# In-place exponentials in PSUM, two-bank PSUM tiles and two chunks per group in an RWKV6 + Hyena kernel

## The chip, the cores and the metric

The kernel runs on one core of a Trainium2 chip. The metric is device time in microseconds (us) of one execution. Every run is compared with runs of the kernel before on the same chip. Executions carry a state: "slow" is a run that is more than 1.5% above the fastest of its kernel; verdicts use the fast runs alone. The engines are PE (matrix multiplies), DVE (VectorE), ACT (ScalarE), POOL (GpSimd) and SP (which issues DMAs here).

## The reference

Stage one is RWKV6 attention with a state; stage two takes its output through a projection, a long convolution in the frequency domain, gates and an output projection. Cut to what matters:

```python
B, H, S, D = 4, 8, 768, 48
for t in range(S):                                    # stage one
    cur = einsum('bhd,bhe->bhde', u[None] * kt, vt)   # the "bonus" of the current step
    y[:, :, t] = einsum('bhd,bhde->bhe', rt, state + cur)
    state = wt[:, :, :, None] * state + einsum('bhd,bhe->bhde', kt, vt)
x = y.transpose(0, 2, 1, 3).reshape(B, S, H * D)      # stage two
x1, x2, x3 = split(x @ w_proj)
x2_conv = irfft(rfft(x2) * rfft(filter_fft))
out = (x1 * x2_conv * x3) @ w_out
```

## The kernel before

Stage one runs on 24 chunks of 128 time steps (six per batch). The kernel declares every step as an operation with a due time, its possible engines and the PSUM banks that it takes. A list scheduler in the kernel (`Plan`) then orders them with estimated durations, chooses the banks, and emits the instructions in that order. Its estimates are a model.

The kernel before uses eight banks of PSUM. It declares six of them as six tiles of one bank, and the last two as one tile `sc`, which only the scores use. Cut to one chunk's start and the state update:

```python
NB = 6
bank = [ps.tile([L, 512], FP32, name=f"bank{i}") for i in range(NB)]
sc = ps.tile([L, 2, HP, L], FP32, name="sc")
# ... cut: csi and csx are cumulative sums of log w by PE, each in a bank of its own
op(f"en{i}", T(i, 1.2), [act(C)], lambda e, bk: nc.scalar.activation(
    out=en[f], in_=bank[bk[f"csi{i}"]][:, 0:C], func=AF.Exp, scale=-1.0), w=[f"en.{f}"], uses=[f"csi{i}"])
op(f"ep{i}", T(i, 1.3), [act(C + HP)], lambda e, bk: nc.scalar.activation(
    out=ep[f], in_=bank[bk[f"csx{i}"]][:, 0:C + HP], func=AF.Exp), w=[f"ep.{f}"], uses=[f"csx{i}"])
op(f"kh{i}", T(i, 1.9), [pool(C), dve(C, True)], lambda e, bk: mul(
    e, kh[f][:, :, 0:D], kl[sl], en[f]), ...)
op(f"qh{i}", T(i, 2.0), [pool(C), dve(C, True)], lambda e, bk: mul(e, qh[f][:, :, 0:D], rl[sl], ep[f]...), ...)
# ... cut: transposes, scores, mt = scores * mask; kv = ident @ S + k v on PE; then the new state:
op(f"su{i}", T(i, 4.9), [dve(HP * D)], lambda e, bk: nc.vector.tensor_mul(
    stt[sn], bank[bk[f"kv{i}"]][:, 0:HP * D]..., ep[f][:, C:C + HP].to_broadcast([L, HP, D])), uses=[f"kv{i}"])
```

## Time and profile before

| | kernel before |
|---|---|
| median of the first runs | 179.68 us (179.07 to 182.61) |
| span in the profile | 179.9 us |
| PE / DVE / ACT / POOL busy | 149.2 / 148.7 / 136.5 / 74.3 us |
| DVE idle | 179.9 - 148.7 = 31.2 us |

The page of the profile: first busy time per engine, then busy tenths in 40 slices of 4.5 us, the shares of the engines in the chain of waits that ended last, and one group of instructions (output from inputs, count, busy us, mean ns, idle before them).

```profile
span 179.9 us, 4559 instructions
## 1 busy us (share of the span) xinstructions
PE 149.2 (83%) x1698; PEld 90.5 (50%) x1698; DVE 148.7 (83%) x290; ACT 136.5 (76%) x304; POOL 74.3 (41%) x87
## 2 busy tenths in 40 slices
PE   0553988197999999998999988679999999998761
...
DVE  3899899548979779999997899976799999639650
...
## 4 chain that ended last, share of the span: by engine, by line
PE 49%; DVE 29%; DMA 9%; issue 7%; ACT 2%; POOL 2%; SPq 1%; DVEq 0%; POOLq 0%; ACTq 0%
...
L621 DVE TENSOR_TENSOR sd<-xT 128x384 bf16<-128x384 bf16 x24 | 10.7, 474 | 2.6 <-ACT xT L282 2.4
```

PE and DVE are both over 80% busy, and the chain of waits hops between them. The slices show where it is not so: at the start and after slice 35. Three windows of 40 us say the same in numbers (columns: start:end, length, busy us and instructions of each engine, granted PE clock, DMA share, GB/s):

```profile
core 0: us, PE busy (x) PEld busy (x) DVE busy (x) ACT busy (x) POOL busy (x), PEclk, DMA share, GB/s
0.00:40.00 40.00, 23.77 (x276) 15.97 (x277) 31.38 (x75) 27.00 (x52) 14.52 (x28) 0.87 0.94 196
40.00:80.00 40.00, 37.96 (x451) 23.34 (x449) 36.37 (x68) 33.40 (x79) 18.57 (x20) 1.00 1.02 197
...
160.00:201.00 41.00, 12.54 (x80) 5.81 (x78) 10.88 (x30) 8.62 (x18) 0.00 (x0) 0.96 0.08 29
```

In the first 40 us PE has only 23.8 us of work and the DMA engines are busy throughout: the start waits for loads. In the last 20 us both engines run down. (The span ends at 179.9, so the last window is half empty.)

### The profile page before, as it was taken

What the parts mean: (1) busy time and instruction counts of PE and PEld (TensorE: products, weight loads), DVE (VectorE), ACT (ScalarE), POOL (GpSimd) and SP (SyncE); (2) the same over time, 40 slices, a digit from 0 to 9 for tenths busy, and PEclk for the clock granted to TensorE, in tenths of its full rate; (3) what the DMA queues carried; (4) which work ended last, traced back from release to release, by engine and by line L of the source; (5) the groups of instructions that cost most, each with busy time, mean ns of one, the idle gap of its engine ahead of it and who ended that gap; (6) DMA issues with size and microseconds to landing.
All of it is one profiled execution on the core that took longest, in us unless ns stands there. A gap on an engine that the chain in (4) does not pass through costs nothing.

```text
span 179.9 us, 4559 instructions
## 1 busy us (share of the span) xinstructions
PE 149.2 (83%) x1698; PEld 90.5 (50%) x1698; DVE 148.7 (83%) x290; ACT 136.5 (76%) x304; POOL 74.3 (41%) x87
## 2 busy tenths in 40 slices
PE   0553988197999999998999988679999999998761
PEld 0433765144665663565556744436656556654230
DVE  3899899548979779999997899976799999639650
ACT  4597795378798796899799974949999968686332
POOL 6055632026453454539423992846650562100000
PEclk9999996569999999999999999969999999999998
DMA  5999999699999899999999984467000001500006
GB/s 113 213 219 183 193 299 212 121 211 215 199 173 206 164 213 182 213 206 190 298 176 187 212 175 95 79 168 219 4 2 4 0 4 64 201 5 0 0 31 231
DMA packets 105046, 26.44 MB, mean 147 GB/s; under 512 B 100288, under 2 KB 104640, under 8 KB 105024
## 3 DMA queue, kind: packets, MB, share of 16 engines
q1 hardware_dynamic: 104224, 24.98, 63.5%
q0 software_dynamic: 800, 1.18, 4.0%
q8 instruction: 13, 0.21, 0.5%
q14 instruction: 9, 0.07, 0.1%
HBM read 22.61 MB, written 4.72 MB: 152 GB/s over the span
## 4 chain that ended last, share of the span: by engine, by line
PE 49%; DVE 29%; DMA 9%; issue 7%; ACT 2%; POOL 2%; SPq 1%; DVEq 0%; POOLq 0%; ACTq 0%
DMA r<-in_r_dram 9%; PE bank L594 9%; PE bank L630 7%; PE bank L703 5%; DVE mt L420 4%; DVE U L661 4%; PE bank L516 4%; DVE y L692 3%; PE bank L391 3%; PE sc L414 3%; PE bank L462 3%; DVE eo L689 2%; PE bank L448 2%; DVE P L661 2%; PE bank L509 2%
## 5 line engine op out<-in xcount | busy, mean ns | idle before, releaser
L420 DVE TENSOR_TENSOR mt<-sc,mask_excl 128x1024 bf16<-128x1024 f32 x24 | 29.2, 1218 | 5.2 <-PE sc L414 5.0
L594 PE MATMUL bank<-xT,wproj 128*128 128x384 bf16 x144 | 28.4, 326 | 0.0
L278 POOL TENSOR_TENSOR kh<-k,en 128x384 bf16<-128x384 f32 x16 | 18.4, 1150 | 23.1 <-ACT en L375 21.7
L278 POOL TENSOR_TENSOR vc<-vb,cc 128x384 bf16<-128x384 bf16 x15 | 12.7, 855 | 33.1 <-DVE cc L404 24.7
L278 POOL TENSOR_TENSOR rk<-r,k 128x384 bf16<-128x384 f32 x16 | 17.3, 1078 | 14.9 <-DMA r<-in_r_dram 14.2
L282 ACT ACTIVATE qk<-bank 128x1024 bf16<-128x1024 bf16 x20 | 20.7, 1033 | 2.5 <-PE bank L391 1.8
L278 POOL TENSOR_TENSOR qh<-r,ep 128x384 bf16<-128x384 f32 x17 | 19.5, 1149 | 3.9 <-ACT ep L378 3.9
L703 PE MATMUL bank<-wout,y 128*128 128x384 bf16 x72 | 14.7, 350 | 3.5 <-DVE y L692 3.4
L357 ACT ACTIVATE lg<-w 128x384 bf16<-128x384 f32 x24 | 12.4, 530 | 6.2 <-DMA w<-in_w_dram 6.2
L282 ACT ACTIVATE xn<-bank 128x192 bf16<-128x192 f32 x48 | 13.8, 344 | 4.1 <-PE bank L462 3.6
L594 PEld LDWEIGHTS <-wproj 128*128 128x128 bf16 x144 | 12.5, 97 | 7.0 <-issue 0.3
L363 PE MATMUL bank<-lg,mask_incl 128*128 128x384 bf16 x24 | 8.7, 364 | 8.6 <-ACT lg L357 8.3
L282 ACT ACTIVATE o<-bank 128x384 f32<-128x384 f32 x24 | 11.3, 511 | 5.6 <-PE bank L703 5.5
L630 PE MATMUL bank<-wproj,sd 128*128 128x384 bf16 x72 | 14.2, 326 | 0.9 <-DVE sd L621 0.9
L611 DVE TENSOR_TENSOR g<-bank,x 128x384 bf16<-128x384 f32 x24 | 12.7, 548 | 2.4 <-ACT ab L282 1.6
L282 ACT ACTIVATE xT<-bank 128x384 bf16<-128x384 bf16 x24 | 12.0, 501 | 2.9 <-PE bank L479 2.8
L282 ACT ACTIVATE ev<-bank 128x384 f32<-128x384 f32 x12 | 5.9, 492 | 10.5 <-PE bank L678 10.5
L282 ACT ACTIVATE X<-bank 128x384 bf16<-128x384 f32 x24 | 11.9, 508 | 2.3 <-PE bank L509 1.1
L282 ACT ACTIVATE x<-bank 128x384 bf16<-128x384 f32 x24 | 11.9, 496 | 1.9 <-PE bank L594 1.6
L375 ACT ACTIVATE en<-bank 128x384 f32<-128x384 f32 x24 | 12.0, 500 | 1.2 <-PE bank L363 1.0
L404 DVE TENSOR_REDUCE cc<-rku 128x8 f32<-128x384 bf16 x24 | 12.8, 542 | 0.0
L621 DVE TENSOR_TENSOR sd<-xT 128x384 bf16<-128x384 bf16 x24 | 10.7, 474 | 2.6 <-ACT xT L282 2.4
(102 smaller groups left out, 371.0 us busy)
## 6 DMA issues: line engine op xcount, KB each, us to landing
w<-in_w_dram SPq DMA_DIRECT2D x24, 192.0 KB, 4.0
k<-in_k_dram SPq DMA_DIRECT2D x24, 192.0 KB, 3.9
r<-in_r_dram SPq DMA_DIRECT2D x24, 192.0 KB, 3.9
v<-in_v_dram SPq DMA_DIRECT2D x24, 192.0 KB, 3.8
out_dram<-o SPq DMA_DIRECT2D x24, 192.0 KB, 2.3
filt<-in_moe_filter_fft_dram SPq DMA_DIRECT2D x1, 1152.0 KB, 7.9
wproj<-in_moe_w_proj_dram POOLq DMA_DIRECT2D x1, 864.0 KB, 13.1
wout<-in_moe_w_out_dram POOLq DMA_DIRECT2D x1, 288.0 KB, 4.8
```

Source lines behind the costliest of these rows:

```text
L278: (nc.vector if e == DVE else nc.gpsimd).tensor_mul(o, a, b)
L282: nc.scalar.activation(out=o, in_=a, func=AF.Copy)
L357: op(f"ln{i}", T(i, 0), [act(C, True)], lambda e, bk: nc.scalar.activation(out=lg[f][:, :, 0:D], in_=wl[sl], func=AF.Ln), r=[f"w.{sl}", "t ...
L375: op(f"en{i}", T(i, 1.2), [act(C)], lambda e, bk: nc.scalar.activation(out=en[f], in_=bank[bk[f"csi{i}"]][:, 0:C], func=AF.Exp, scale=-1.0 ...
L404: op(f"cc{i}", T(i, 2.8), [dve(C)], lambda e, bk: nc.vector.tensor_reduce(out=cc[f], in_=rku[f], axis=AX.X, op=ALU.add), r=[f"rku.{f}"], w ...
L420: op(f"mt{i}", T(i, 4.8), [dve(1024)], lambda e, bk: nc.vector.tensor_mul(mt[s2_], sc.rearrange("p q j t -> p (q j) t"), _mid(mask_excl, H ...
L594: nc.tensor.matmul(p, wproj[:, cb, col0:col0 + L], xT[bx][:, cb, sl], start=(cb == 0), stop=(cb == CB - 1),)
L611: op("c" + n3, d + 0.3, [dve(C)], lambda e, bk: nc.vector.tensor_mul(g[bx][:, fb, sl], bank[bk[n3]][:, 0:HALF], x1[0][:, fb, sl]), r=[f"x1 ...
L621: op(f"sd{b}.{q}.{ti}", d, [dve2(C, True)], lambda e, bk, q=q, fn=fn: fn(sd[q][:, :, sl], lo, hi), r=[f"xT.{bx}.{ti}", f"xT.{bx}.{NT + ti} ...
L630: nc.tensor.matmul(bank[bk[n]][:, 0:C], sd[q][:, cb, ti * L:(ti + 1) * L], wproj[:, cb, C:2 * C], start=(cb == 0), stop=(cb == CB - 1),)
L661: lambda e, bk, o=o, a=a, c=c, fn=fn: fn(tl(o)[:, sl, :], tl(a)[:, sl, :], tl(c)[:, sl, :]),
L703: nc.tensor.matmul(bank[bk[n]][:, 0:C], y[cb][:, ti * L:(ti + 1) * L], wout[:, cb, :], start=(cb == 0), stop=(cb == CB - 1),)
```

## The change

The intent: fewer and larger instructions, and a shorter chain per chunk. Both exponentials become one ACT instruction of 768 elements that writes over the cumulative sums in PSUM. One DVE multiply then reads k's and q's factors from there and takes k and r (`kq`), in place of two multiplies of 384 on POOL or DVE. To let one instruction span two banks, PSUM is declared as four tiles of two banks. Loads and the first elementwise steps take two chunks as a group (the first two groups have one chunk each, the third and all later ones two). For six of the 13 groups the bonus is made by transposes and small matmuls on PE instead of a DVE reduction. Priorities are tuned anew and the projection weights are loaded after chunk 1's logarithm, not chunk 4's. The core of the diff, with cuts marked:

```diff
-    NB = 6
-    bank = [ps.tile([L, 512], FP32, name=f"bank{i}") for i in range(NB)]
-    sc = ps.tile([L, 2, HP, L], FP32, name="sc")
+    bank = [ps.tile([L, 2, 512], FP32, name=f"bank{i}") for i in range(4)]
+    def one(bk, n):                       # a step that needs one bank: one half of a pair
+        i, m = bk[n]
+        return bank[i // 2][:, i % 2, :]
+    def two(bk, n):                       # a step that needs two: a whole pair
+        i, m = bk[n]
+        return bank[i]
# ... cut
+        def exps(e, bk):
+            p = two(bk, f"cs{i}")
+            nc.scalar.activation(out=p[:, :, 0:C], in_=p[:, :, 0:C], func=AF.Exp)
+            nc.scalar.activation(out=phi[f], in_=p[:, 1, C:C + HP], func=AF.Exp)
+        op(f"kq{i}", T(i, O_KH), [dve(2 * C)], lambda e, bk: nc.vector.tensor_mul(
+            kq[f][:, :, :, 0:D], two(bk, f"cs{i}")[:, :, 0:C]..., kr[sl][:, :, q]), ...)
# ... cut
+            op(f"su{i}", T(i, O_SU), [dve(HP * D)], lambda e, bk: nc.vector.tensor_mul(
+                stt[sn], one(bk, f"kv{i}")[:, 0:HP * D]..., phi[f].to_broadcast([L, HP, D])), uses=[f"kv{i}"])
# ... cut: projections, forward transform, outputs in pairs of banks (one eviction of 768); bonus on PE
-PACE = 5.021
-WP, WO, FL = 4, 9, 5
+PACE = 4.317
+WP, WO, FL = 1, 7, 3
```

In the scheduler each of the eight banks still has a time of its own at which it comes free. A step of one bank may take a half of a pair whose other half is in use.

## The prediction

> **What bounds it now.** The span is 179.9 us. By the table of busy times PE is busy 149 us, DVE 149, ACT 136, POOL 74. The chain of waits hops between PE (49%) and DVE (29%). By windows, between 20 and 150 us DVE is over 90% busy in most stretches and PE 92-100%: a co-limited steady state. The losses are at the ends. From 0 to 40 us PE is busy only 24 us and the DMA share is 0.85-0.98. After 160 us DVE is busy 11 of 20 us. In all, DVE is idle 31 us. Part of its busy time is stretching: sums of bf16 tiles in SBUF take 0.35 us at the median but up to 1.15 when POOL runs (mean 0.47 for sd).
>
> **What the change does, by engine** (durations from the groups by form, 384 -> 768 elements interpolated between the 384 and 1024 forms).
> - DVE: kh and qh (15 multiplies on DVE, 33 on POOL) become 24 multiplies of 768 elements on DVE alone, about 0.95 us each: 22.8 us for 9.8. Given back: rku goes from 24 DVE operations to 3, cc from 24 reductions to 7 double ones (12.8 -> 6.5 us), vc and rk from 17 to 4 double ones, paired g. Added: 9 xT copies (0.35 us), 3 rx, 3 qk. sd now reads one operand from PSUM; the Trainium skill ("VectorE: DVE Perf Modes", "The perf-mode tier table") lists tensor_tensor with any PSUM operand at 1x, so I cost it at 0.35 to 0.55 us, not less. Uncontended, DVE work grows some 4 to 8 us; POOL falls from 74 to about 55 us, so stretching shrinks by about as much. Net DVE busy 145-152 us: no relief.
> - ACT: 300 activations become about 205. Two exponentials (0.50+0.52 us) become one of 768 in place (about 0.8) plus a tiny one (about 0.2); pairs of 384 evictions (2x0.50) become one of 768 (about 0.8). ACT busy 136 -> 120-126 us.
> - PE: the same matmuls plus 30 transposes (8 take 0.45 us) and 30 matmuls of 8 columns: +2 to 3 us.
> - POOL no longer stands between the exponentials and the transposes: two POOL multiplies of 1.15 us in series become one DVE multiply. Waits of POOL on en (21.7 us) and on cc (24.7 us) mostly disappear.
> - Dues are spaced 4.32 us per chunk, not 5.02. Exponentials hold a bank pair until the multiply, but all eight banks circulate.
>
> **On the critical path.** No busy engine gets much less work, so the gain must come from idle time: a shorter chain per chunk (about 1.5 us), a faster start, fewer fixed costs, and at the end output matmuls started before the last y (18 now wait for it, 2.8 us). I expect DVE idle to fall from 31 to about 17-20 us: span about 149 + 18 = 167. Against it: the last batch's tail (21 us after its last sums) stays serial.
>
> Predicted 166.5 us, 8 in 10 between 159 and 175. Faster by over 2%: 0.88; within 2%: 0.08; slower: 0.04.
>
> **Right if** the profile shows DVE busy 145-152 at 88% or more of the span, ACT 120-126, POOL about 55; the 768 multiply about 0.95 us; first 40 us with more PE work than 24 us; tail after the last sums no longer than 21 us.
>
> **Wrong if** in-place exponentials run slow in PSUM; bank pairs held from matmul to multiply starve PE; three group buffers delay loads (ACT waiting on w); the delayed second stage of early batches piles up behind the last chunk so that the tail grows; or the throttle cuts the denser PE stream (granted 0.74 between 20 and 40 us already).

## More of the kernel before

What DVE waits for, by instruction (line, releaser, us in total, times, longest):

```profile
engine line waited for: us in total, times, longest us
DVE mt L420 <- PE sc L414: 5.0, 7, 1.2
...
DVE S L440 <- PE bank L433: 2.2, 3, 1.1
...
DVE S L440 <- PE bank L456: 1.5, 1, 1.5
```

The releasers of the state update `S` are real ones: line 433 is the accumulation `kv` that it reads, and line 456 reads an older state from the tile that `S` writes. Its waits are short, 3.7 us in all. The view by line has this total, and beside it the projection's matmuls, which wait for nothing:

```profile
L594 PE MATMUL bank<-xT,wproj 128*128 128x384 bf16 x144 | 28.4, 326 | 0.0
...
L440 DVE TENSOR_TENSOR S<-bank,ep 128x192 bf16<-128x192 f32 x20 | 7.0, 349 | 3.7 <-PE bank L433 2.2 <-PE bank L456 1.5
```

## The result, and the profile after

The change made the kernel slower: 204.25 us median (202.48 to 206.17) against 179.68 (179.07 to 182.61), a ratio of 1.135 with a 95% interval of 1.125 to 1.145. Ratios here are the mean time of one kernel's fast runs over that of the other's fast runs of the same rounds, so they are not quite the ratio of the quoted medians. The profile shown here is of a repeat (e4 below: median 203.29 us; the profiled execution took 204.55).

The page of the change, same parts as before:

```profile
span 201.5 us, 4435 instructions
## 1 busy us (share of the span) xinstructions
PE 156.7 (78%) x1758; PEld 97.1 (48%) x1758; DVE 144.5 (72%) x248; ACT 127.3 (63%) x208; POOL 50.6 (25%) x57
## 2 busy tenths in 40 slices
PE   0572657798798874989579994789889998999960
...
DVE  1529524728496759998679999968798797979660
...
## 4 chain that ended last, share of the span: by engine, by line
PE 45%; DVE 23%; ACT 13%; DMA 7%; issue 5%; SPq 4%; ACTq 0%; DVEq 0%
...
L498 DVE TENSOR_TENSOR kq<-bank,kr 128x768 bf16<-128x768 f32 x24 | 22.5, 949 | 5.9 <-ACT phi L494 5.9
...
L493 ACT ACTIVATE bank<-bank 128x768 f32<-128x768 f32 x24 | 19.2, 802 | 4.9 <-PE bank L489 4.8
...
L544 DVE TENSOR_TENSOR S<-bank,phi 128x192 bf16<-128x192 f32 x20 | 7.1, 354 | 10.8 <-PE bank L506 2.7
...
L593 DVE TENSOR_TENSOR sd<-xT,bank 128x384 bf16<-128x384 bf16 x24 | 7.5, 348 | 8.4 <-ACT xT L333 4.4
...
L333 ACT ACTIVATE ab<-bank 128x768 bf16<-128x768 f32 x12 | 9.7, 810 | 4.5 <-PE bank L742 4.4
```

PE is busy 7.5 us longer and DVE 4 us less, but DVE idle went from 31.2 to 201.5 - 144.5 = 57.0 us. The single instructions cost what was expected: `kq` 949 ns, exponentials of 768 in place 802 ns. So the loss is waiting. The windows of the change:

```profile
core 0: us, PE busy (x) PEld busy (x) DVE busy (x) ACT busy (x) POOL busy (x), PEclk, DMA share, GB/s
0.00:40.00 40.00, 21.43 (x236) 15.30 (x236) 19.10 (x42) 21.98 (x33) 12.86 (x33) 1.00 0.98 184
40.00:80.00 40.00, 31.71 (x429) 20.85 (x426) 26.71 (x42) 26.21 (x47) 15.70 (x10) 1.00 1.02 207
...
160.00:201.00 41.00, 33.77 (x298) 18.48 (x296) 28.95 (x61) 21.75 (x34) 0.00 (x0) 1.00 0.16 58
```

DVE loses most in the first 80 us: 45.8 us busy against 67.8. That work moves to the end: after 160 us DVE still has 29 us to do, against 11. What DVE waits for now, those of `S` alone:

```profile
DVE S L544 <- PE bank L506: 2.7, 3, 2.1
DVE S L544 <- PE bank L704: 2.7, 3, 1.3
...
DVE S L544 <- PE bank L581: 2.0, 2, 1.9
```

The state update `S` waits 10.8 us in all, against 3.7, and the names are odd. Lines 506, 704 and 581 are transposes of k and q, a gate's projection, and transposes of the output: none of them is an input of `S`. They write other banks.

I therefore compared, in the built programs, every semaphore wait on PE with the last PE instruction that really touches the same bytes. In the kernel before, none of DVE's 82 waits and none of ACT's 236 names a later instruction than that. In the change 29 of DVE's 59 and 47 of ACT's 133 do: they name the last PE instruction that wrote anywhere in the same two-bank tile. Of the 15 waits of `S` on PE, 11 are too late in this sense. I call them false waits. Not all of them lie between two steps: 5 of the 29 and 20 of the 47 only wait for the last small matmuls of their own step, and they stay in e2 below. False waits also go the other way. Of the waits of PE's matmuls that write a bank, 21 on DVE and 16 on ACT name a later instruction than the bytes need (none in the kernel before): PE then waits for a reader of the other half.

Theory A: the false waits, which the scheduler does not know of, make the loss. Rivals: B, two-chunk groups start the pipeline late; C, the bonus on PE; D, the early load of the weights; E, the new order or work itself.

### The profile page after: what moved, and what is told of

Read it like the earlier page. It is cut to its first block, busy times and chain, and to the rows that moved or that the text cites. A ratio compares the mean times of both kernels' runs of the same rounds, so it can differ in the third digit from the quotient of the medians.

```text
span 204.1 us, 4435 instructions
## 1 busy us (share of the span) xinstructions
PE 161.2 (79%) x1758; PEld 98.4 (48%) x1758; DVE 145.2 (71%) x248; ACT 127.8 (63%) x208; POOL 50.7 (25%) x57
## 4 chain that ended last, share of the span: by engine, by line
PE 49%; DVE 19%; ACT 13%; DMA 6%; SPq 6%; issue 5%; ACTq 0%; DVEq 0%
PE bank L704 6%; PE bank L627 5%; SPq L425 5%; DMA w<-in_w_dram 5%; ACT qk L333 5%; PE bank L506 4%; PE bank L742 4%; PE bank L821 4%; DVE U L778 4%; DVE mt L524 3%; PE bank L620 3%; PE bank L789 2%; PE bank L793 2%; DVE sd L593 2%; PE bank L581 2%
## 5 line engine op out<-in xcount | busy, mean ns | idle before, releaser
L329 POOL TENSOR_TENSOR vc<-vb,cc 128x768 bf16<-128x768 bf16 (+1 forms) x11 | 15.1, 1369 | 82.7 <-DVE cc L445 23.6
L524 DVE TENSOR_TENSOR mt<-bank,mask_excl 128x1024 bf16<-128x1024 f32 x24 | 29.2, 1216 | 1.3 <-PE bank L518 1.3
L498 DVE TENSOR_TENSOR kq<-bank,kr 128x768 bf16<-128x768 f32 x24 | 22.5, 949 | 5.7 <-ACT phi L494 5.6
L329 POOL TENSOR_TENSOR rk<-kr 128x768 bf16<-128x768 f32 (+1 forms) x11 | 19.1, 1736 | 14.9 <-DMA kr<-in_r_dram 9.1
L493 ACT ACTIVATE bank<-bank 128x768 f32<-128x768 f32 x24 | 19.2, 802 | 3.9 <-PE bank L489 3.4
L506 PE MATMUL bank<-ident,kq 128*128 128x128 bf16 x192 | 16.8, 238 | 3.2 <-DVE kq L498 2.7
L333 ACT ACTIVATE xn<-bank 128x384 bf16<-128x384 f32 x24 | 11.6, 489 | 7.3 <-PE bank L566 7.3
L506 PEld LDWEIGHTS <-kq 128*128 128x128 bf16 x192 | 13.4, 107 | 5.3 <-DVE kq L498 3.5
L333 ACT ACTIVATE x<-bank 128x768 bf16<-128x768 f32 (+1 forms) x16 | 10.4, 649 | 7.4 <-PE bank L704 6.1
L731 DVE TENSOR_TENSOR g<-bank,x 128x768 bf16<-128x768 f32 (+1 forms) x16 | 11.9, 749 | 0.2 <-PE bank L465 0.2
```

Of the source, the lines that this page charges most:

```text
L329: (nc.vector if e == DVE else nc.gpsimd).tensor_mul(o, a, b)
L333: nc.scalar.activation(out=o, in_=a, func=AF.Copy)
L493: nc.scalar.activation(out=p[:, :, 0:C], in_=p[:, :, 0:C], func=AF.Exp)
L498: op(f"kq{i}", T(i, O_KH), [dve(2 * C)], lambda e, bk: nc.vector.tensor_mul(kq[f][:, :, :, 0:D], two(bk, f"cs{i}")[:, :, 0:C].rearrange("p ...
L506: nc.tensor.transpose(p[:, HP * m + j, :], kq[f][:, m, 2 * j:2 * j + 2, :], ident)
L524: op(f"mt{i}", T(i, O_MT), [dve(1024)], lambda e, bk: nc.vector.tensor_mul(mt[s2_], two(bk, f"sc{i}").rearrange("p a (j t) -> p (a j) t", ...
```

## The experiments

All kernels gave correct results. The kernel before ran in 179.68 to 181.81 us (medians). The medians below are of all executions, slow ones too; the ratios are of fast ones alone. In order of the argument:

| label | what | median us | ratio to before (95%) |
|---|---|---|---|
| e4 | the change again | 203.29 | 1.124 (1.118 to 1.131) |
| e2 | the change, eight one-bank tiles, pair operations cut in two | 191.54 | none given |
| e13 | the same cut operations, on two-bank tiles | 206.46 | 1.136 (1.126 to 1.145) |
| e1 / e8 | before, six banks as three two-bank tiles | 221.0 / 220.02 | 1.220 / 1.223 (1.217 to 1.230) |
| e9 | before, one pair of banks as one tile | 195.85 | 1.085 (1.071 to 1.099) |
| e3 | the change, a step of one bank takes a whole pair | 190.02 | 1.051 (1.045 to 1.056) |
| e5 | e3, one chunk per group | 193.02 | 1.075 (1.069 to 1.081) |
| e6 | e3, bonus on DVE | 192.92 | 1.076 (1.070 to 1.082) |
| e7 | the change, bonus on DVE | 202.67 | 1.118 (1.113 to 1.124) |
| e10 | before, weights early | 190.27 | 1.045 (1.030 to 1.059) |
| e11 / e17 | the change, three pairs and two single banks, tuned | 184.8 / 185.22 | 1.025 / 1.031 (1.025 to 1.036) |
| e12 | e11, weights later, tuned | 189.68 | 1.052 (1.047 to 1.056) |
| e14 / e16 | e11, bonus on DVE, tuned | 184.57 / 184.7 | 1.014 / 1.030 (1.024 to 1.037) |
| e15 | the change, eight single banks, tuned | 188.9 | 1.034 (1.022 to 1.045) |

"Tuned" means that the priorities were searched again on the scheduler's own plan for that arrangement.

### e4: the change again

No edit, on the chip of the other runs.

> The changed kernel once more, for a profile in the fast state and for the rounds beside the others: both theories say 201-205 us.

Measured: 203.29 us (202.83 to 204.55). The result stands.

### e1 and e8: the kernel before on shared tiles

```diff
-    bank = [ps.tile([L, 512], FP32, name=f"bank{i}") for i in range(NB)]
+    pairs = [ps.tile([L, 2, 512], FP32, name=f"bank{i}") for i in range(NB // 2)]
+    bank = [pairs[i // 2][:, i % 2, :] for i in range(NB)]
```

Nothing else changes: same operations, same order, same bank numbers.

> The kernel before, unchanged in operations, order and bank numbers; only its six PSUM banks are declared as three tiles of two banks instead of six of one. Theory A (false waits: the framework tracks a two-bank tile as one, so a reader of one bank also waits for the last matmul into the other): in the built program 22 of 58 DVE waits and 78 of 173 ACT waits on PE now name a later PE instruction than the data needs, against none before, so the time rises from 180 to 188-198 us. Theory B (the change is slow because of its order and of fewer, larger steps, not of waits): 179-181 us, no change.

Measured: 221.0 us (220.15 to 290.32; the 290 was a slow run and the profiled one). That is above even theory A's range of 188 to 198: the loss is two to five times what was expected. In the slow run the projection's matmuls took 541 ns on average, against 351 in the repeat, at a granted clock of 1.0; what slowed them stays open, and nothing is concluded from it. The run was repeated for a profile:

> The kernel before with its banks declared in pairs, again, for a profile in the fast state: the profiled run of the first time was a slow one (288 us). 219-222 us.

Measured: 220.02 us. The declaration alone costs the kernel before some 40 us. What DVE waits for in e8:

```profile
DVE S L441 <- PE bank L704: 4.0, 2, 2.3
...
DVE g L612 <- PE bank L480: 3.3, 1, 3.3
DVE S L441 <- PE bank L679: 2.8, 1, 2.8
```

The same odd names appear as in the change: `S` waits for output projections (704) and inverse transforms (679), and a gate's product `g` for line 480, transposes of the attention output. `S` waits 15.2 us in all, against 3.7 with the same order on one-bank tiles. (Lines are one higher than in the kernel before.) PE waits too. The projection's matmuls, which never waited before, now sit idle 5.7 us behind ACT:

```profile
L595 PE MATMUL bank<-xT,wproj 128*128 128x384 bf16 x144 | 32.1, 351 | 5.7 <-ACT qk L283 3.3 <-ACT ep L379 1.0 <-ACT X L283 0.6
...
L441 DVE TENSOR_TENSOR S<-bank,ep 128x192 bf16<-128x192 f32 x20 | 7.1, 355 | 15.2 <-PE bank L704 4.0 <-PE bank L679 2.8 <-PE bank L434 2.0
```

### e9: one pair only

```diff
+    pair = ps.tile([L, 2, 512], FP32, name="pair")
+    bank = [pair[:, i, :] for i in range(2)] + [ps.tile([L, 512], FP32, name=f"bank{i}") for i in range(2, NB)]
```

> The kernel before with only its banks 0 and 1 declared as one tile, the other four as tiles of their own: a smaller dose of the same. In the built program 8 of 70 DVE waits and 26 of 209 ACT waits on PE are later than needed (three pairs: 22 of 58 and 78 of 173, +40 us). The theory of false waits: +8 to +18 us, 188-198 us. If the loss with three pairs came from something else that needs all of them: under 183 us.

Measured: 195.85 us, ratio 1.085. One shared tile, with the other four banks apart, already costs some 15 us (8.5%), within the 8 to 18 that theory A expected. With three it is some 40 (22%).

### e2 and e13: the change's operations with and without shared tiles

e2 declares eight one-bank tiles and cuts each instruction on a pair in two. Order and bank numbers stay.

```diff
-    bank = [ps.tile([L, 2, 512], FP32, name=f"bank{i}") for i in range(4)]
+    bank = [ps.tile([L, 512], FP32, name=f"bank{i}") for i in range(8)]
-            nc.scalar.activation(out=p[:, :, 0:C], in_=p[:, :, 0:C], func=AF.Exp)
+            for z in (0, 1):
+                nc.scalar.activation(out=p[z][:, 0:C], in_=p[z][:, 0:C], func=AF.Exp)
# ... likewise kq, mt, xn, and every eviction or product on a pair
```

> The changed kernel in the same order on every engine and with the same bank numbers, but with eight one-bank tiles; each operation that took a pair of banks is cut in two, one per bank. False waits on PE fall from 47 to 20 (ACT) and from 29 to 5 (DVE); ACT and DVE pay some 100 more fixed costs. Theory A: 184-194 us in spite of those. Theory B: 203-210 us, as the order is the same and the fixed costs rise.

Measured: 191.54 us (188.13 to 193.31). Three of the four runs count as slow; the one fast run, 188.13, is too little for a ratio. But the slowest of the four is 9.5 us below the fastest of the change in the same call. Here two things changed, the tiles and the number of instructions. So e13 keeps e2's instructions and takes the tiles back:

```diff
-    bank = [ps.tile([L, 512], FP32, name=f"bank{i}") for i in range(8)]
+    pairs = [ps.tile([L, 2, 512], FP32, name=f"bank{i}") for i in range(4)]
+    bank = [pairs[i // 2][:, i % 2, :] for i in range(8)]
```

> Control for the run with eight one-bank tiles (191.5 us): the same instructions, cut in two, in the same order on the same bank numbers, only that the eight banks are again declared as four two-bank tiles. The built program has 46 of 59 waits of DVE on PE and most of those between PE and the other engines later than needed. If false waits within a shared tile are the cause, the time is 203 us or more (the change as given: 203.3; the cut operations add instructions, so up to 212). If the cut itself or something else made that version faster, it stays at 191 to 195 us.

Measured: 206.46 us (205.03 to 207.95). With the same instructions in the same order on the same banks, the shared tiles cost 206.46 - 191.54 = 14.9 us by the medians, and 18.3 against e2's one fast run: 15 to 18 us. (The two ran in different calls; the kernel before was at 181.67 and 181.27 us in them.) e13 has more false waits than the change (46 of DVE's 59 waits on PE, against 29 of 59), so this is not quite the change's own loss. Nor is it shown that cutting the instructions costs anything on shared tiles: e13 is 3.2 us above e4, but the intervals of their ratios overlap.

One state update shows it. In e13 (first DVE, then PE; columns: start, us, engine, line, operation, and idle before):

```profile
start us, us, engine line op out<-in xcount [idle before <-releaser]
...
62.71 1.01 DVE L502 TENSOR_TENSOR kq<-bank,kr 128x384 bf16<-128x384 f32 x2
64.93 0.36 DVE L555 TENSOR_TENSOR S<-bank,phi 128x192 bf16<-128x192 f32 x1 [1.21 <-PE bank L718]
```

```profile
63.02 0.31 PE L548 MATMUL bank<-vb,kq 128*64 128x48 bf16 x8
...
64.24 0.65 PE L718 MATMUL bank<-xT,wproj 128*128 128x384 bf16 x3
```

`S` needs line 548 (`kv`), which ended at 63.02 + 0.31 = 63.33. DVE came free from `kq` at about 63.7. But `S` started at 64.93, behind line 718, a gate's projection, which ended at 64.24 + 0.65 = 64.89: 1.21 us lost. The same place in e2:

```profile
57.65 1.01 DVE L501 TENSOR_TENSOR kq<-bank,kr 128x384 bf16<-128x384 f32 x2
58.58 0.35 DVE L554 TENSOR_TENSOR S<-bank,phi 128x192 bf16<-128x192 f32 x1
```

```profile
57.38 0.31 PE L547 MATMUL bank<-vb,kq 128*64 128x48 bf16 x8
...
58.60 0.65 PE L717 MATMUL bank<-xT,wproj 128*128 128x384 bf16 x3
```

Here `S` (58.58) follows `kq` directly, and line 717, the same projection, only starts at 58.60 and waits for nobody: in the built program it writes the bank beside the one that `S` reads, and both run at once. (The profiled run of e2 was a slow one, its granted clock 0.952; e13's, a fast one, had 0.955.) Over all 20 state updates, e13 and then e2:

```profile
L555 DVE TENSOR_TENSOR S<-bank,phi 128x192 bf16<-128x192 f32 x20 | 7.1, 353 | 9.2 <-PE bank L512 3.0 <-ACT qk L334 1.8 <-PE bank L718 1.7
```

```profile
L554 DVE TENSOR_TENSOR S<-bank,phi 128x192 bf16<-128x192 f32 x20 | 7.0, 349 | 1.1 <-PE bank L547 1.1
```

9.2 us of waiting become 1.1, and no releaser but `kv` is left. `S` is one link of a chain: the next chunk's `kv` needs it.

### e3: a step of one bank takes the whole pair

Pairs stay, but no two steps share one: a step of one bank occupies the whole pair, and the scheduler knows it.

```diff
-        avail = [0.0] * (2 * self.npairs)
+        avail = [0.0] * self.npairs          # written out: nsing = 0 single banks + the pairs
-        return bank[i // 2][:, i % 2, :]
+        return bank[-1 - i][:, 0, :]
```

> The changed kernel, its pairs kept, but a step that needs one bank takes a whole pair, so that no two steps share a tile; the order is planned anew under that scarcity (the kernel's own plan grows from 167 to 173 us). Theory A: 188-198 us, faster than the change in spite of the scarcity. Theory B: 205-212 us.

Measured: 190.02 us, ratio 1.051, in theory A's range. Half as many places in PSUM, and 13 us faster than the change. The scheduler's plan for e3 ends at 172.7, the change's at 167.0: the plan thought it 5.7 us slower. The windows show where the time comes back. From 40 to 80 us DVE is busy 35.8 us (e2: 33.1), against 26.7 in the change and 36.4 before. In the first 40 us it is not: 19.2 (e2: 21.2), against 19.1 and 31.4. So the 12 us that DVE lacks there are not due to false waits.

### e5, e6, e7: groups and bonus

e5 is e3 with one chunk per group (rival B); e6 and e7 put the bonus on DVE, in e3 and in the change (rival C).

```diff
-NLD, NF, NG, NS, NO = 3, 3, 2, 2, 5
+NLD, NF, NG, NS, NO = 6, 3, 4, 2, 5        # e5, with its loads, lists of groups, bonus, and WO, FL = 12, 5
-BONUS = "p" * NBP + "d" * (13 - NBP)
+BONUS = "d" * 13                           # e6, e7
```

> The previous kernel of this series (the change, a one-bank step taking a whole pair, 190.0 us), with one chunk per group in place of two: loads, logs, bonus and copies of v come in single chunks, with six load buffers of one chunk, so the same bytes. Its own plan is 172.9 us, as before (172.7). If the rest of the loss (9 us against the kernel before) comes from the doubled groups (a group can start only when both chunks are there; DVE was busy only 19 us of the first 40, against 31 in the kernel before), the time falls to 181-186 us and DVE is busy over 24 us of the first 40. If it does not: 188-193 us.

Measured: 193.02 us; DVE busy in the first 40 us 20.6 (e3: 19.2), where B wanted over 24. Single chunks do not bring the start back, and B falls, as far as e3's arrangement shows it (the priorities were not searched again).

> The kernel with a one-bank step taking a whole pair (190.0 us), with the bonus of every chunk on DVE and none on PE: 30 transposes, 30 small matmuls and their one-bank steps go, DVE gains some 6 us of work. Its own plan is 176.0 us, 3.3 longer. If the bonus on PE costs more than it saves (it takes two banks per group): 185-189 us. If it is neutral or good: 190-195 us.

> The change as it is, shared pairs and false waits included, with the bonus of every chunk on DVE: fewer one-bank steps share pairs (ACT waits on PE later than needed 48 of 132, DVE 24 of 66, against 47 of 133 and 29 of 59). The theory of false waits says they stay and so does the time: 201-209 us (plan 172.5 against 167.0). If the PE bonus were the cause: 180-188 us.

Measured: e6 192.92, 2.9 us slower than e3; e7 202.67 against 203.29 of the change, from different calls, with ratios whose intervals overlap. (Two of e7's four runs were slow.) C, which wanted 180 to 188, does not explain the loss.

### e10: weights early in the kernel before

```diff
-WP, WO, FL = 4, 9, 5
+WP, WO, FL = 1, 9, 5
```

> The kernel before with the load of the projection weights asked for after chunk 1, as in the change, not after chunk 4; nothing else by hand, but the plan reorders: its own end goes from 160.3 to 164.1 us. If early weights and an order that is not the tuned one make the rest of the loss (9 us): 183-187 us. If they do not matter on the chip: 179-182 us.

Measured: 190.27 us (187.94 to 192.1), ratio 1.045 from two fast runs, 187.94 and 188.75. Both expected ranges lie below it. In an order that was tuned for late weights this costs much, so D stayed a candidate for a part.

### e11: three pairs and two single banks

The change's operations; a step of one bank takes a single bank or a whole pair, so nothing shares a tile. Priorities tuned for it, and with them the choice of groups whose bonus is on PE (seven of the 13).

```diff
-    bank = [ps.tile([L, 2, 512], FP32, name=f"bank{i}") for i in range(4)]
+    bank = [ps.tile([L, 2, 512], FP32, name=f"bank{i}") for i in range(3)]
+    single = [ps.tile([L, 512], FP32, name=f"single{i}") for i in range(2)]
```

> The change's operations with three tiles of two banks and two of one bank; a one-bank step takes a one-bank tile or a whole pair, so no tile is shared; its priorities and its choice of chunks for the bonus on PE searched anew with its own plan (168.2 us, against 176.5 before the search and 172.7 of the kernel of 190.0 us). The plans that do not share tiles have come out about 17 us over their plan: 183-188 us. If the plan says nothing of the chip: 188-196 us.

Measured: 184.8 us (184.66 to 184.97), ratio 1.025: 18.5 us below the change, the best of its kind, still not faster than the kernel before.

### e12: the same, weights later

```diff
-WP = 1
+WP = 3          # and the priorities searched again
```

> The change's operations with three two-bank tiles and two one-bank tiles as in the fastest version so far (184.8 us), but with the projection weights loaded after the logarithm of chunk 3 instead of chunk 1 (the kernel before: chunk 4), and the priorities searched again for that. Its own plan ends at 170.1 (the fastest version's: 168.2). Theory, early weights make the remaining 2.5%: [...] the gap between chip and plan shrinks from 16.6 to under 14 and the time is below 183.5 us; DVE busy in the first 40 us rises from 22.2 to over 26. Rival, the remaining 2.5% lie in the change's work and in the banks that are left: the gap stays at 16 to 18 and the time is 186 to 188.5 us.

Measured: 189.68 us (189.3 to 190.06), with DVE busy 24.6 us in the first 40. Both ranges missed it: it is slower than either theory expected. Later weights did not help in this order, so D is not supported as the cause of the rest. It is not a clean test: all priorities differ from e11's, and the granted clock was 0.930 to 0.957 against e11's 0.975 to 0.997.

### e14, e16, e17: the same, bonus on DVE

```diff
-BONUS = 'ddpdppppdpdpd'
+BONUS = 'd' * 13     # and the priorities searched again, among them WP = 2, not 1
```

> The version with three two-bank and two one-bank tiles, with the whole bonus on DVE, priorities searched again (its own plan ends at 166.2; with the bonus partly on PE 168.2, which ran in 184.8). If the bonus on PE is what the remaining 2.5% are, PE busy falls from 152.5 to 148 to 150 and the time to 180 to 183 us. If it is not, DVE takes the work with no gain and the time is 184 to 188 us.

Measured: 184.57 us (182.64 to 188.59, the last a slow run), ratio 1.014 (1.004 to 1.024). The interval overlapped with e11's (1.017 to 1.033), so both ran again together, with more rounds:

> Mixed tiles, bonus on DVE. If the bonus on PE is what remains, this is within 1% of the kernel before (ratio under 1.01) and at least 2 us faster than the next run. If it is not, it is 1.5 to 2.5% slower than the kernel before and within 1 us of the next run.

> Mixed tiles, bonus partly on PE. Both theories expect what it gave before, a ratio of 1.02 to 1.03; it is here to be compared with the run before it on the same chip.

Measured: 184.7 and 185.22 us, ratios 1.030 and 1.031: no difference. (Both lie just above the ranges expected, 1.5 to 2.5% and 1.02 to 1.03.) The page of e16:

```profile
span 181.5 us, 4317 instructions
## 1 busy us (share of the span) xinstructions
PE 147.2 (81%) x1698; PEld 91.4 (50%) x1698; DVE 146.1 (81%) x237; ACT 128.1 (71%) x208; POOL 61.5 (34%) x59
```

PE makes the same 1698 matmuls as in the kernel before and is busy 2 us less, DVE 2.6 us less. The time is still longer, with DVE idle 181.5 - 146.1 = 35.4 us. So PE's extra work is not what remains. Nor is DVE's: in e17, with more of the elementwise work on POOL, DVE is busy only 131.9 us, and the time is the same.

### e15: eight single banks, tuned

As e2, but the cut operations may take any two free banks, the second instruction is charged in the plan, and the priorities are tuned.

> The change with eight one-bank tiles, every operation on two banks cut in two and allowed any two free banks, the second instruction charged in the plan, priorities searched again (its plan ends at 167.8). If taking and giving back two banks together costs the remaining 2.5%, this version gains them in spite of some 100 more instructions: under 183 us. If not, the fixed cost of the cut instructions shows and the time is 184 to 188 us.

Measured: 188.9 us (186.59 to 192.33), ratio 1.034 from two fast runs, 186.59 and 188.28; their mean, 187.4, is in its "if not" range. Taking two banks at once is not shown to be the rest either: what it may save, the further instructions may cost.

## Why the prediction was wrong

- **The instructions: right, or off by little.** `kq` 0.949 us (predicted about 0.95), ACT busy 127.3 (120 to 126), DVE busy 144.5 (145 to 152), POOL 50.6 (about 55). PE gained 7.5 us of busy time where 2 to 3 were expected; in e3, with the same matmuls, it gained 3.4, so the rest is not the matmuls themselves.
- **The step that failed: "Exponentials hold a bank pair until the multiply, but all eight banks circulate."** In the scheduler they do. In the program that was built, a wait on a bank is a wait on its two-bank tile. 29 of DVE's 59 waits on PE name a later instruction than the bytes need, and `S` waits 10.8 us in place of 3.7. On equal instructions sharing the tiles costs 15 to 18 us (e13 against e2). The converse holds in the kernel before: the declaration alone costs 40 us for three pairs and 15 for one. The risk "bank pairs held from matmul to multiply starve PE" was near, but it was not the holding: e3 holds whole pairs for every small step and is 13 us faster.
- **The sum that followed: "I expect DVE idle to fall from 31 to about 17-20 us: span about 149 + 18 = 167."** It rose to 57.0. And even where nothing shares a tile it did not fall: 35.4 in e16. So this was a hope that no chain in the trace supported, and without false waits the prediction would still have missed: e11 took 184.8, not 159 to 175. The "faster start" did not come: PE was to have more than 24 us of work in the first 40, and had 21.4. In the kernel before and in all versions whose windows I read (the change, e11, e12, e16) the DMA share there is 0.94 to 0.98 and PE busy 21 to 25 us. It looks as if loads bind the start, which the change does not shorten; no run tests this.
- **The tail** was to be no longer than 21 us after the last sums. It was 201.5 - 175.7 = 26 us. The prediction named a longer tail among its risks, and the false waits did not make it: where no two steps share a tile it is about as long (e2 25.6, e3 24.9, e16 29.8, counted the same way). The change's loss against e3 lies before the last sums.
- **POOL's waits on `cc`** (24.7 us) were to mostly disappear. They grew: 22.6 us on DVE's reductions and 38.5 on the copies of `cc` from PSUM by DVE and ACT. But POOL is busy a quarter of the span and is not in the chain that ended last.

The account of the 22 us between the change and the kernel before (203.29 against 181.27): sharing the tiles costs 15 to 18 on cut instructions; tiles unshared and an order made for it together give back 18.5 in e11. What remains is some 3% in the best versions (e16, e17: about 5 us). Late weights (e12), the bonus (e16 against e17) and paired banks (e15) did not remove it; one chunk per group was only tried in e3's arrangement. The scheduler's plan is no guide to these 5 us: it ends at 166.2 for e16 and 160.3 for the kernel before. That the rest is the changed work in an order that is not as good was only argued; it stays open. No version beat the kernel before.

That the chip itself does not need the false waits is seen from the runs on one-bank tiles: correct, with neighbouring banks in use. The Trainium skill ("PSUM — Partial Sum Buffer", section "PSUM bank collisions raise a hardware error") says that collisions concern one bank and a quarter of its partitions, and that accesses to different banks run clean. The correct results of e2 and e15 agree, and so does the place in e2 shown above, where DVE reads a bank from 58.58 us while PE writes the one beside it from 58.60.

## What to carry to other kernels

A tile that spans two banks is one object to what places the waits: if two steps use its halves at once, each can wait for the other's last instruction, readers and writers alike. Take a pair whole or declare its banks apart, and give the scheduler the same rule as the program. When a new wait names an instruction that is not an input, look at what shares its tile, before costing instructions any finer. And do not book a fall in idle time unless the trace shows which chain gets shorter, and that this chain is the one that binds.

## What the Trainium skill lacked or had wrong

- "Perfetto Trace Analysis", section "Optimization Strategy", says that consistent bubbles can mean that there is not enough PSUM or SBUF for the next tile. Here bubbles came from waits on the other half of a shared tile: e3 with half the places is 13 us faster than the change. The page lacks this cause; its sign in the trace is a releaser that is no input.
- No page that I read gives the cost in waits of a PSUM tile of two banks: +15 us for one pair, +40 us for three (e9, e8), +15 to 18 us in the change's own order (e13 against e2).
- "VectorE: DVE Perf Modes", section "The perf-mode tier table", lists `tensor_tensor` with any PSUM operand at 1x. Here a 384-element bf16 sum with one bf16 operand in PSUM took 348 ns on average, while a 384-element product with an f32 PSUM operand took 548 ns; both operands in SBUF took 0.35 us at the median, but 474 ns on average and up to 1151, where the sum with the PSUM operand stayed within 340 to 355. That fits the same page's section "Why PSUM operands drop a tier", which caps at 2x_1P, and 1x for fp32.
- "ScalarE: Activation LUTs", section "Step-by-step: what each stage is for", says that ScalarE is faster to PSUM than to SBUF. Exponentials of 768 in place in PSUM took 802 ns, evictions of 768 to SBUF 810 ns: 1% (the functions differ, and the page gives no size).
